# Stripe attention on one core: x of the row pairs is blocked in DRAM and turned by DMA, output stores choose their queue, and the order of steps is a new one

## The chip, the cores and the metric

The kernel runs on one core of one Trainium2 chip. The metric is the device time of one execution, in microseconds; the time before is the median of three runs. A profile is a separate execution, which gives each instruction of each engine with its start and duration: TensorE (PE, its weight loads PEld), VectorE (DVE), ScalarE (ACT), GpSimd (POOL) and the queues of SyncE (SP) and ScalarE (ACTq) that issue DMAs.

## The reference

An image of 224 x 224 positions with 96 channels is projected to q, k and v. The first 48 channels attend within horizontal stripes of 8 rows, the last 48 within vertical stripes of 8 columns; each stripe has 8 x 224 = 1792 tokens, and there are 28 stripes each way. Both results are put together and projected by wo.

```python
qkv = jnp.einsum('bhwc,cd->bhwd', x, wqkv)          # x: 1, 224, 224, 96
q, k, v = qkv[..., :C], qkv[..., C:2*C], qkv[..., 2*C:]
qh = q[..., :C2].reshape(B * nh, sw * W, C2)         # horizontal stripes, C2 = 48
ah = softmax(einsum('bqc,bkc->bqk', qh, kh) * C2 ** -0.5)
oh = einsum('bqk,bkc->bqc', ah, vh).reshape(B, H, W, C2)
...                                                  # qv, kv, vv, ov: the same with vertical stripes
o = concatenate(oh, ov)                              # written as a sum of two padded arrays
return jnp.einsum('bhwc,cd->bhwd', o, wo)
```

All arrays are bfloat16.

## The kernel before

The 56 stripes are worked in 28 pairs P: pairs 0 to 13 are horizontal (row pairs, phase 0), 14 to 27 vertical (phase 1). The two stripes w of a pair share the partitions: one stands on rows 0 to 63 of QT and KT, the other on rows 64 to 127.

**One pair.** The queries come in four chunks of 512, 512, 512 and 256, the keys in 14 tiles of 128. A score tile is 128 keys x 512 queries of both stripes (in the last chunk 256 keys x 256 queries), 1024 columns over two PSUM banks; a pair has 49. For 41 of them ACT takes the exponential out of PSUM into a tile `PT` (`emit_qk`, activation at L798; scores by `qk_fn`, L635). The other eight go another way (`emit_s`, L648): DVE and POOL work out the exponential by polynomials in 16-bit numbers (L836, L838, L841 on DVE, L848 to L852 on POOL), through buffers `qb`. `emit_pv` (L661) multiplies each `PT` with V into a PSUM bank; a column of ones in V gives the sums. When a chunk is complete, DVE copies it to `OT_sb` (L815).

**Work in between ("fills").** Matmuls with a DVE eviction each, through a ring of four PSUM banks:
- `prep_fills(P)` prepares the next pair from `xT_sb[P % 2]`, x with channels on the partitions and a row of ones at row 96. In phase 0 come first four T fills: each turns eight blocks of 112 tokens from `x_sb` by TensorE (L437, two transposes a block, so 16 matmuls), and DVE copies the bank into `xT_sb` (L443), where it also brings the tokens into the order of 8 x 8 blocks that the vertical phase needs. Then four K fills (L454, L459), one small QB fill (L483, L487), four Q fills (L454, L470) and three V fills (L501, L508). The first K fill needs all four T fills.
- `fin_fills(P)` multiplies `OT_sb` with wo and divides by the sums (L537, L544, L552 in phase 0, into `Ph_sb`; L573, L580, L585 in phase 1, which add `Ph_sb` and write `out_sb`).

**x.** `plan_x` (phase 0) loads a pair's x in four DMAs into `x_sb`, which lies in the memory of `out_all`; it is issued when the last T fill of the pair before has read `x_sb` (`emit_fill`). `keep_x` stores the turned x of each horizontal pair to `xt` in DRAM; in phase 1 `plan_x` loads a vertical pair's x from there, already turned. `x_sb` has a 97th column of ones, so that the row of ones is turned with it. Pair 0 has a way of its own, with x in `x0_sb` and steps written out one by one (`t_lead`, `lead_pe`, `lead_ev`).

**Output.** Each of the 392 DVE results of phase 1 (L585) is stored by a DMA of 24 KB, issued on SP (`emit_evict`). Once the last exponential has been put into the program, stores go by turns to SP's and ACT's queue (`tail_q`).

**Order.** The program is written as one list of steps, `ORDER`, a string for each pair: q is a score tile for ACT, 1 and 2 the two passes of a tile of DVE and POOL, v a PV step, k the next prep fill, f the next fin fill. PE runs them in exactly this order. A planner inside the kernel (`dve_step`, `pool_step`, with constants such as `D_ACT` and `D_H`) decides from modelled times in which order DVE and POOL take what PE hands them, and which bank and buffer each step gets. `x_t[P]` is the time from which the planner takes a pair's x to be there. `S.commit` and `dma` append each instruction with the semaphores that it must wait for. `queue_prep(P)` is called at the first score tile of pair P - 1: it issues that pair's DMAs on SP and puts the prep fills of pair P in their queue. SP works strictly in the order of issue: an instruction that waits holds all that stand behind it.

The lines that issue and choose:

```python
        for c in "".join(ORDER):
            if c == "q":
                do_q()
            elif c in "12":
                do_s(c)
            elif c == "v":
                do_v()
            else:
                do_fill(c)
```

Of the kernel before, what the change touches and what calls it, by code (L numbers as in the profile page):

```python
# [5 lines left out]
BF16 = mybir.dt.bfloat16  # L6
FP16 = mybir.dt.float16
FP32 = mybir.dt.float32
# [24 lines left out]
SEMD, SEMP, SELF, SEMX = 0.15, 0.10, 0.19, 0.05  # L33
D_H, D_SQ, D_AF, D_ML = 0.608, 1.9, 1.03, 2.08
# [9 lines left out]
    "kkqqkkkq1qkkq1qq1kqvqkvvq1vqvkqkq1qkvq2vqkq1vqvvqvq2qvkq2qkvqkvvvq1qvkvqkvvq1kqv2qkqvkvq2qvvkqkq2vqvkqv1qvvkqvv2qkqvv",  # L44
    "fqkkqkfqvq1vvkqq2vvvq1vvqvvqv2qvvqvvq1q2vqkvvq1qvkvqffqvkqv1qkvvqkqv2qvkqkvq1qvvqk2qvvvq1qvvffqvvq2qkvqkvq2vkqvq2vvqv1qvvqkvfq",
    "v1qvvq1vqvvqkvqkq2vqvvq1vqvkq1qvq1vqvvvqvkq2qvvvq1vqkkqvv2qkvqvfqv2qvvq2vkqvvkq2qvvkvqkq1vvq2qvvvkqffqvvkqv2qvvvqkqvkvfqffqvvkvq2qvvvv",
    "1qvvq1qvvvq1vqvvqkqvkq1qfvvqv1qkqkq2qfvkqkqfkqvq2vqfvvq1qvvvqvvq2vkqvq1vvq2qvvvvq2qvvkvq2qvvvkvq1qvvvkq2qvvkqkqkvvkqffqvvkvvq2fqv",
    "vvq1qvvvq1vqkvq1qkvqvvqfvqkqv1qkq2fqvvqvkvq2vqv1qvq2vkqq1vqvkqvvvqkvq2kqvvq1qvkvqkqkkqfvq2qvkqvvkq2vqv1qkvqv1qvvvqvfqv1qvv",
    "2qvvq1vvqvqvvkq2qvkqkvqffqvvvvq2qvvkqv1q1qvvvq2qvkvqkvq1vqvvvqv2qvqkkvqv1qkfqvkvqkfqvvq1vqv2qvvq2vqvfqv2qvkqkvvq2qvvkqv1qkvqvvkqffvv",
    "q2qvkvqfvq1vqvvq1fqvvvqvvq1qvkqv2qfqvvq1vvq1vqkqvvqkq2vqv1qvq2vqkvkqkvqkvq2vqvvq2kvq1qvvkvq2qvvkvq1qvkvqkvvqf2qvvvqvkqkvfqv2qkv",  # L50
    "vq1qv1qvvqvvfqvqfkqkqk2qvqkvfqv1qvvq1vqv1qvvqvkqvfqvvq2vvkqvq2vqvkq2vvvq2qvvvkvq1qvkfqv2qvfqkvqkvkq1qvvkqvkq2vqv1qvvvq1qvvkvq2qvkv",
    "vvq1qvvvvqvqkfqkvqvvq1q2qvq2vqkqvfq1vqvkqfqvv2qvqv1qkvvqvqvkqvkvqvkq2qvvfqvvq1qkfqvvkq1vqv2qvfqvkqvkvq2qvkvqkvqk1qvvvvq2qvvvk",
    "vq2qkqkv1qvq1qvvkqvfqvvvvq1qvvv1qvqf2qvvvvq2qvkvq1qvkqvvqvv2qkqkvvkqvq1kqvvffqvvq2vqvkq1qvvkq2qvvkq2qkvqvkkqvvq2fqvvvqv1qfvqvvkq1",
    "fqvvkvqq2vkvqvq1vvqvvq2qvqvvq1qv2qkqkq1q1qvvqvvvfqfqvkvvqkvkqfvkvqq2kvv1qqvvkvvq2qvvkvq2qvvvq1vvq2qkvqkkvqv2qvvqvfqvvkq1qkvvq1vfqvv",
    "q2vqv1qvkqvqkqkvqv1qvq2vqv2qvkqfvqfvvq1qvvkqkkvqv1qvvqvkqvvq2kq1qvvvq2qvkqv2qvvfqfvqkqkkvq1qvkvqvkq2vfqvkqvvvqf1qvvvq2vvq2vvq",
    "ffqvvvq1vqvkfqvvqv1qvkqvqvvq2vqkvq1qkfqvvqkq1qvvkq2vqvkqkfqkvvq2vqkvq1kqvvqkqvvfqvvqv2qvvq1vvqkq2vqv2qkvvq1qvkvvq2qvvvfqkvqkvvvq1f",
    "qvvvvq2vqvqfvvvq1vq1qvqvvq1qv2qvvqkv1qvkq2qvvq1vqvkqqvvqvv2qvfqkqvk1q2qvvq2qfvqvkvq2qkvvq1qvv1qkqkvvq1qvkkqvvvq1qkvvvqvvq2v",
    "qvfqvv2qvfqvvq1vqvvq1vqv2qvvqvkq1vqvkvqvvqvkqkvfqv2qvvq2vqvvq2vqvfqkvq1vqkvqvkq2vqvkq1qvv2qvkqvkq1qvvvq1kqvvkqvfqv2qvvq2vqv1qv",
    "vvqvvvqffqvvvvq2qvv1qvvqv1qkqkqvkqfkqvfqvkqvkq2qkqv2qvvq1vqvkqvvqkvq2qvvq1fqvvqfvvqv2qvqv1qfvvq2qvkqvq1vqvkvq1qvfqkvvvq2qvvv",
    "q2fqvvvqvfqvvqvv1qqvvqvv1qfqvvq2vvqq1vvq2qkvkqkqv2qkvvq1qkvvqvvq2qvvq1fqvvkqvqkvq1vfqvvq2vqkqvv2qvqkkqv2qvvvvq2qvvvkq1qkvvq1vf",  # L60
# [3 lines left out]
    "1qvvvqvvq2qfqv1qvvqvvvq1vqv1qvvqvvqvfq1qvvqvvkq2qvv2qvvq2qvkqkvkqv2qkvqkq1vqvkq2vqvkq2vfqvqkvqfvvqv2qvvq1qvvkqvkqfvq2qvvfqk",  # L64
    "vqv2qvvq1q1qvvvqvvq1fqvqvvvvq1qvvkvqkvq2qkvfqvkqvvq2vvqffqvvqvvvqv2qkqf2qvqvvkq1qvvvqvqkvq1vqvkq2vqkkqkvq1qvvvqfkqvv2qvvq1vq",
    "1qvvqv2qfvqvq1vqvvqvvvqv1qfqq2vqvvkq2vqvq1fqvvvq2vqvkqv1qkvqvvqkvvqv1qkq2kqvvq2qvvkq1qkvvq1vqfkqvq2vqvkqkvq2vqvvkq1qvv1q",
    "fqvvvqvvq1qvvfqvvq2vqv1qvvqv2qvvq2vvqv2qkq1qvvfqvqvkqvvvq1vqv2qvvq2vqvvq1fqvvqkvkqvfqvkvq2qkvvvq1qfvvvq2qvvkqkqkvvvq2qvkvvqkvq1kqv",
    "ffqvvqfqvvqv1qvvvqvvq1vqvqv2qkvvqkvqfvqv2qvvq1vqv2qvvkqkvfqvqkvq1vqvkqvvqv1qfqv2qvqv1qvq2vfqvvq2vqkqkvvqv1qvq2vqkkvq1qvkqvkv",
    "q2fqvvvqv1qqvvfqvqvvvq1qvvvq1vqkvqkq1vvqvqvv2qkqkvvq2vqv2qvq1vvqfqk2qvvqkqkkvq2qvvfqvvvq2qvv1qfqvkvqvvq2qvkvvq1qvvvkq1qfvvqfvk",
    "qvfqvq2vvq1qvqvvvq1qvvvqfvq2qvvvq1qvvkqkvq2vqv2qvfqkvqkvvq2vvqvvq2qv1qfqvvvqkqv1qvfqvvvq2qvkqkq1vkqkqvq2vfqvvvq1qvvkvq1qkvk",  # L70
    "vq2qfvqvvq1vvqqvv1qvvqv1qvvq2q2qfvqvvq1vvqvqvvq2vfqvvq1vqvqv1fqvqvvvq2qvvq2vfqvvvq2vqfvfqvqvvfqvvffqvvfqvq2vfqvvvq2fqvvfqvvqvqfffvvvvvvfff",
# [101 lines left out]
def bass_standalone__window_attn_cswin__vision_kernel(  # L173
# [28 lines left out]
    with es:  # L202
# [19 lines left out]
        xT_sb = [sb(f"xT_sb{i}", [C + 1, 2, NTOK], BF16) for i in range(2)]  # L222
# [12 lines left out]
        x_sb = out_all[0:TH, 0:2 * NTH * (C + 2)].rearrange("p (w k c) -> p w k c", w=2, k=NTH)  # L235
# [18 lines left out]
        for b in range(2):  # L254
            for w in range(2):
                SEMS[f"x{b}{w}"] = sem(f"s_x{b}{w}")
            SEMS[f"out{b}"] = sem(f"s_out{b}")
            SEMS[f"xt{b}"] = sem(f"s_xt{b}")
        dma_tot = {k: 0 for k in SEMS}
# [71 lines left out]
        pool_now(["xone"], lambda e: e.memset(x_sb[:, :, :, C:C + 1], 1.0), 0.25)  # L331
# [27 lines left out]
        xt = nc.dram_tensor("xt_dram", [WB, C, NTOK], BF16).ap()  # L359

        def ph_of(P):
            return 0 if P < NPH else 1

        def plan_x(P):
            for w in range(2):
                if ph_of(P) == 0:
                    i = 2 * P + w
                    src = x_flat[i * NTOK:(i + 1) * NTOK, :].rearrange("(k p) c -> p k c", p=TH)
                    for hf in range(2):
                        dma("sp", [], [("x", w, hf)], x_sb[0:TH, w, hf * FTH:(hf + 1) * FTH, 0:C],  # L370
                            src[:, hf * FTH:(hf + 1) * FTH, :], f"x{w}{hf}")
                else:
                    b = P % 2
                    dma("sp", [("xt", i) for i in range(NPH)], [("xT", b, w)], xT_sb[b][0:C, w, :],
                        xt[2 * (P - NPH) + w], f"x{w}{b}", lat=4.5)
# [16 lines left out]

        flags = set()
# [31 lines left out]
        def prep_fills(P):  # L425
# [3 lines left out]
            for w in range(2 if ph == 0 else 0):  # L429
                for hf in range(2):  # L430
                    k0 = hf * FTH

                    def pe_fn(e, bk, w=w, k0=k0):
                        bkb = bk.bitcast(BF16)
                        for j in range(FTH):
                            for a, z in HALVES:
                                ins = e.transpose(bkb[a:z, j * TH:(j + 1) * TH], x_sb[0:TH, w, k0 + j, a:z], ident[0:TH, 0:TH])  # L437
                        return ins

                    def d(e, bk, w=w, hf=hf):  # L440
                        src = bk.bitcast(BF16)[0:C + 1, 0:FTH * TH].rearrange("c (r bc dw) -> c r bc dw", r=RPF, dw=8)
                        dst = xT_sb[b][0:C + 1, w, :].rearrange("c (bc r dw) -> c r bc dw", r=SW, dw=8)[:, hf * RPF:(hf + 1) * RPF, :, :]
                        return e.tensor_copy(dst, src)  # L443
                    pd, dd = 0.42, 0.53
                    T.append(fill("B", pd, pe_fn, [("x", w, hf), "ident", "xone"],
                                  [(dd, d, [], [("xT", b, w)], None)], [], ("T", P, w, hf)))
            for kind, L in (("k", K), ("q", Q)):
                for c in range(NCH):
                    q0, qs = CH_Q0[c], CH_SIZES[c]

                    def pe_fn(e, bk, kind=kind, q0=q0, qs=qs):
                        for w in range(2):
                            lw = w_sb[:, wblk(P, "k"), :] if kind == "k" else wq_sb[ph][b][:, w, :]
                            ins = e.matmul(bk[64 * w:64 * w + 64, 0:qs], lhsT=lw, rhs=xT_sb[b][:, w, q0:q0 + qs],  # L454
                                           start=True, stop=True)
                        return ins
                    if kind == "k":
# [5 lines left out]
                        needs = [("T", P, w, hf) for w in range(2) for hf in range(2)] if c == 0 and ph == 0 else []  # L463
                        if P >= 2:
                            needs = needs + [("PV", P - 2)]
# [26 lines left out]
            for k0 in range(0, 2 * NKT, VS):  # L492
# [12 lines left out]
                def d(e, bk, k0=k0, n=n):  # L505
# [5 lines left out]
                              [("T", P, w, hf) for w in ws for hf in range(2)] if ph == 0 else [], ("V", P, k0)))  # L511
# [81 lines left out]

        tail_q = [0]
# [167 lines left out]
        plan_x(1)  # L762
        p_left = {}

        def queue_prep(P):
            if P <= NPH:
                keep_x(P - 1)
            if P == NPH:
                plan_x(P)
            if NPH <= P < NP - 1:  # L770
                plan_x(P + 1)
            T, K, QB, Q, V = prep_fills(P)
            fl = T + K + [QB] + Q[:1] + V + Q[1:]
            if P in (1, NPH - 1):
                fl = [wqT_fill(P // (NPH - 1))] + fl
            prep_q.extend(fl)
            p_left[P] = len(T)
# [9 lines left out]
        def emit_fill(f, bi):  # L787
            S.commit("pe", 0.0, f["pe_dur"], f["pe_dur"] + L_FILL, lambda e, fn=f["pe_fn"], bk=bank(bi): fn(e, bk),
                     f["reads"], [("bank", bi)], fresh=[("bank", bi)])
            g = f["gives"]  # L790
            if g[0] == "T":
                p_left[g[1]] -= 1
                if p_left[g[1]] == 0 and g[1] + 1 < NPH:
                    plan_x(g[1] + 1)
# [23 lines left out]
        def emit_evict(f, bi, k):  # L818
# [374 lines left out]
```

## Time and profile before

| | us |
|---|---|
| median of three runs (1088.88 to 1089.72) | 1088.9 |
| the profiled execution | 1089.64 |
| span of its trace, first to last instruction | 1087.8 |
| ACT busy (98%) | 1067.8 |
| PE busy (97%) | 1057.2 |
| DVE busy (96%) | 1044.7 |
| POOL busy (88%) | 954.9 |
| first exponential of the pairs starts (from the span's start) | 9.10 |
| last exponential ends | 1078.36 |

The span is what the trace shows of the engines; the time of an execution has 1.84 us around it. Busy time counts an engine as busy whenever at least one of its instructions is under way, and neighbouring instructions overlap (a matmul or an activation is begun before the one before has ended), so a busy share says less than the step from one start to the next. TensorE's granted clock was full throughout the pairs. The DMA engines were busy for about a fifth of the span.

Of the DMAs, by line, with the median time from issue to landing: the loads of x in phase 0 (52 of 168 KB) took 3.0 us, the stores of turned x (26 of 336 KB, in pieces of 128 bytes) 5.4, its loads in phase 1 (28 of 336 KB) 3.9, the output stores (392 of 24 KB) 1.9.

### The profile page before, as it was taken

Reading aid. Unit: us, or ns where it says so; the run is one execution under the profiler, and the core shown is the slowest. Engines: PE = TensorE matmul, PEld = TensorE weight load, DVE = VectorE, ACT = ScalarE, POOL = GpSimd, SP = SyncE. Lnnn points to the kernel's source line nnn. Section 1 sums busy time; section 2 is a strip of 40 time slices with the busy share of each in tenths; the row PEclk is TensorE's granted clock in tenths of the full one; section 3 lists DMA queues with packets and bytes.
Section 4 is the critical chain, followed back from the end, with each engine's and each line's share of the span. In section 5 each row is a group of like instructions: output and inputs, shape, how many; then the busy total and the mean of one; then the engine's idle time right before and its main releaser. Section 6 shows DMA issues by size and latency. Waiting matters only on the chain. (4 is left out here: it accounts for less than half of the span.)

```text
span 1087.8 us, 36152 instructions
## 1 busy us (share of the span) xinstructions
PE 1057.2 (97%) x14928; PEld 428.0 (39%) x14928; DVE 1044.7 (96%) x2298; ACT 1067.8 (98%) x1159; POOL 954.9 (88%) x597
## 2 busy tenths in 40 slices
PE   9999999999999999999999999999999999999996
PEld 4433444444343444444334333333333333333332
DVE  8999999999999999999999999999999999999997
ACT  8999999999999999999999999999999999999996
POOL 7999788899888988987999888998987999798894
PEclk9999999999999999999999999999999999999998
DMA  5413023202302311311011111112111111211102
GB/s 95 67 25 53 16 38 52 48 14 46 53 15 40 53 33 22 54 28 52 2 27 29 29 45 45 41 22 49 40 42 28 45 39 20 49 43 21 25 19 39
DMA packets 183805, 40.97 MB, mean 38 GB/s; under 512 B 180408, under 2 KB 180952, under 8 KB 183640
## 3 DMA queue, kind: packets, MB, share of 16 engines
q1 hardware_dynamic: 182520, 38.17, 18.2%
q8 instruction: 117, 1.92, 0.7%
q10 hardware_dynamic: 1120, 0.49, 0.2%
q14 instruction: 48, 0.39, 0.1%
HBM read 19.36 MB, written 19.27 MB: 36 GB/s over the span
## 5 line engine op out<-in xcount | busy, mean ns | idle before, releaser
L798 ACT ACTIVATE PT<-ps 128x1024 bf16<-128x1024 f32 x1148 | 1063.5, 1064 | 6.9 <-PE ps L635 4.4
L635 PE MATMUL ps<-QT_sb,KT_sb 49*64 49x512 bf16 (+1 forms) x5420 | 477.6, 362 | 13.9 <-ACT PT L798 8.2
L661 PE MATMUL ps<-PT,V_sb 128*49 128x512 bf16 (+1 forms) x3136 | 459.8, 361 | 0.3 <-DVE PT L841 0.2
L848 POOL TENSOR_TENSOR PT<-qb 128x1024 f16<-128x1024 f16 x168 | 316.6, 1893 | 71.2 <-DVE qb L836 29.0
L852 POOL TENSOR_TENSOR PT<-PT,qb 128x1024 f16<-128x1024 f16 x168 | 355.6, 2126 | 8.9
L841 DVE SCALAR_TENSOR_TENSOR PT<-ps,PT 128x512 uint16<-128x512 f32 x448 | 291.2, 682 | 12.9 <-PE ps L648 7.0
L836 DVE TENSOR_SCALAR qb<-ps 128x512 f16<-128x512 int16 x448 | 291.1, 682 | 10.1 <-PE ps L648 7.2
L635 PEld LDWEIGHTS ps<-QT_sb,KT_sb 49*64 49x64 bf16 x5420 | 144.8, 104 | 286.0 <-ACT PT L798 254.9
L661 PEld LDWEIGHTS ps<-PT,V_sb 128*49 128x49 bf16 x3136 | 133.5, 103 | 201.1 <-issue 158.8
L851 POOL TENSOR_SCALAR PT<-PT 128x1024 f16<-128x1024 f16 x168 | 175.3, 1043 | 14.3
L648 PE MATMUL ps<-QT_sb,KT_sb 50*64 50x512 bf16 (+2 forms) x1792 | 178.8, 389 | 5.7 <-DVE PT L841 1.5
L850 POOL TENSOR_TENSOR PT<-PT 128x1024 f16<-128x1024 f16 x56 | 106.0, 1893 | 20.3 <-DVE PT L838 13.3
L585 DVE SCALAR_TENSOR_TENSOR out_all<-ps,rc,Ph_sb 128x96 bf16<-128x96 f32 x392 | 96.6, 307 | 0.4
L648 PEld LDWEIGHTS ps<-QT_sb,KT_sb 50*64 50x64 bf16 (+2 forms) x1792 | 51.1, 104 | 64.7 <-DVE qb L836 14.4
L838 DVE SCALAR_TENSOR_TENSOR PT<-ps,qb 128x512 f16<-128x512 int16 x112 | 72.8, 680 | 0.1
L815 DVE CAST OT_sb<-ps 113x512 bf16<-113x512 f32 x112 | 68.9, 615 | 1.0 <-PE ps L661 0.2
L470 DVE CAST QT_sb<-ps 128x512 bf16<-128x512 f32 (+1 forms) x111 | 67.5, 614 | 0.9 <-PE ps L454 0.3
L459 DVE TENSOR_SCALAR_CACHE_REDUCE KT_sb<-ps 128x512 bf16<-128x512 f32 x108 | 64.4, 615 | 0.5 <-PE ps L454 0.2
L552 DVE TENSOR_TENSOR Ph_sb<-ps,rc 128x480 bf16<-128x480 f32 (+1 forms) x84 | 51.9, 617 | 1.4
L508 DVE CAST V_sb<-ps 128x480 bf16<-128x480 f32 (+1 forms) x84 | 50.5, 619 | 1.4 <-PE ps L501 0.9
L454 PE MATMUL ps<-xT_sb,w_sb 97*64 97x512 bf16 x224 | 40.8, 365 | 0.3 <-DVE PT L838 0.2
L454 PE MATMUL ps<-xT_sb,wq_sb 97*64 97x512 bf16 x224 | 40.7, 363 | 0.0
(63 smaller groups left out, 393.1 us busy)
## 6 DMA issues: line engine op xcount, KB each, us to landing
xT_sb<-xt_dram SPq DMA_DIRECT2D x28, 336.0 KB, 3.9
out_dram<-out_all SPq DMA_DIRECT2D x386, 24.0 KB, 1.9
out_all<-in_x_dram SPq DMA_DIRECT2D x52, 168.0 KB, 3.0
xt_dram<-xT_sb SPq DMA_DIRECT2D x26, 336.0 KB, 5.4
xt_dram<-xT_sb SPq DMA_DIRECT2D x4, 168.0 KB, 4.8
Ph_sb<-in_x_dram SPq DMA_DIRECT2D x2, 168.0 KB, 3.4
Ph_sb<-in_x_dram ACTq DMA_DIRECT2D x2, 168.0 KB, 3.7
out_dram<-out_all ACTq DMA_DIRECT2D x6, 24.0 KB, 1.9
```

Source lines behind the costliest of these rows:

```text
L454: ins = e.matmul(bk[64 * w:64 * w + 64, 0:qs], lhsT=lw, rhs=xT_sb[b][:, w, q0:q0 + qs], start=True, stop=True)
L585: return e.scalar_tensor_tensor(out_sb[b][:, w, kt, :], bk3[:, s, 0:C], rc[ri][:, s:s + 1], Ph_sb[:, kt, j, :], ALU.mult, ALU.add)
L635: ins = e.matmul(bank(SETS[s] + w)[64 * kh:64 * kh + 64, i * t["qs"]:(i + 1) * t["qs"]], lhsT=KT_sb[b][64 * w:64 * w + CA, kt * 128 + 64 * ...
L648: ins = e.matmul(bank(bp[w])[64 * kh:64 * kh + 64, 0:512], lhsT=KT_sb[b][64 * w:64 * w + nr, kt * 128 + 64 * kh:kt * 128 + 64 * kh + 64], ...
L661: ins = e.matmul(bank(pb)[64 * w:64 * w + CA, 0:t["qs"]], lhsT=V_sb[b][:, w, kt, :], rhs=PT[slot][:, ca:ca + t["qs"]], start=st and i == 0 ...
L798: S.commit("act", 0.0, D_ACT, None, lambda e, s=s, slot=slot: e.activation(PT[slot][:], ps[:, 512 * SETS[s]:512 * SETS[s] + 1024], ACTF.Ex ...
L836: fn, reads, writes = lambda e: e.tensor_scalar(q, low16(bi), m, a, ALU.mult, ALU.add), bk, qk
L841: fn, reads, writes = lambda e: e.scalar_tensor_tensor(y.bitcast(U16), bank(bi), 128.0, y.bitcast(FP16), ALU.mult, ALU.add), bk + ptk, ptk
L848: sq = lambda e: e.tensor_tensor(y, q, q, ALU.mult)
L850: return [("pool", D_SQ, lambda e: e.tensor_tensor(y, y, y, ALU.mult), yk + ["pser"], yk)]
L851: af = lambda e: e.tensor_scalar(y, y, PB, 128.0 * PA, ALU.add, ALU.mult)
L852: ml = lambda e: e.tensor_tensor(y, y, q, ALU.mult)
```

## The change

- **x of pairs 1 to 13.** `block_x` copies a stripe from DRAM to DRAM (`xp`), so that the tokens stand in the order of 8 x 8 blocks, in pieces of 1536 bytes. `load_x` loads it into `x_sb`, now 128 partitions x 14 blocks x 128 columns for each stripe, of which the DMA fills 96; the other 32 are ones, written once. `turn_x` turns it with one DMA transpose for each stripe, from `x_sb` into `xT_sb`, whose tile now has 128 rows. The T fills are gone, and with them what waited for them (`t_t`, `t_n`, `p_left`).
- **When.** `queue_prep` issues, on SP, the transposes of a pair one pair ahead, its load before that and its block copy before that. Pairs 1 and 2 are issued in the lead; pair 1's transposes stand on SP behind the loads of wo.
- **Stores.** `tail_q` is replaced by two modelled times, `tm["sp"]` and `tm["aq"]`, each store counting `D_ST`; after the last exponential a store goes to ACT's queue if that one is free earlier by them.
- **Order.** 22 of the 28 strings of `ORDER` are new; each has 41 q as before.
- The share of tiles between ACT and the other two engines (`KINDS`, `KIND_OF`), all score, PV, K, Q, V and output matmuls, and all DVE and POOL operations on them stay. Counted in the built programs, PE has 832 matmuls fewer (the transposes), DVE 52 copies fewer; SP has 26 block copies, 26 loads and 26 transposes where it had 52 loads.

```diff
-        xT_sb = [sb(f"xT_sb{i}", [C + 1, 2, NTOK], BF16) for i in range(2)]
+        xT_sb = [sb(f"xT_sb{i}", [128, 2, NTOK], BF16) for i in range(2)]
...
-        x_sb = out_all[0:TH, 0:2 * NTH * (C + 2)].rearrange("p (w k c) -> p w k c", w=2, k=NTH)
+        x_sb = out_all[:, 0:2 * NKT * 128].rearrange("p (w k c) -> p w k c", w=2, k=NKT)
...
-        pool_now(["xone"], lambda e: e.memset(x_sb[:, :, :, C:C + 1], 1.0), 0.25)
+        pool_now(["xone"], lambda e: e.memset(x_sb[:, :, :, C:].rearrange("p w k c -> p (w k) c").bitcast(FP32), pair_of_ones), 0.5)
...
+        xp = nc.dram_tensor("xp_dram", [2, 2, WB, SW, 8 * C], BF16).ap()
...
+        def block_x(P):
+
+            for w in range(2):
+                src = x[0, (2 * P + w) * SW:(2 * P + w + 1) * SW].rearrange("r (b d) c -> b r (d c)", d=8)
+                dma("sp", [], [("xp", P % 2, w)], xp[P % 2, w], src, f"xp{P % 2}{w}")
+
+        def load_x(P):
+            for w in range(2):
+                src = xp[P % 2, w].rearrange("b r (d c) -> (b r d) c", d=8).rearrange("(k p) c -> p k c", p=128)
+                dma("sp", [("xp", P % 2, w)], [("x", w)], x_sb[:, w, :, 0:C], src, f"xl{w}")
+
+        def turn_x(P):
+            b = P % 2
+            for w in range(2):
+                reads, writes = [("x", w), "xone"], [("xT", b, w)]
...
+                def fn(eng, w=w):
+                    return eng.dma_start_transpose(xT_sb[b][:, w, :].rearrange("c (k p) -> c k p", p=128),
+                                                   x_sb[:, w, :, :].rearrange("p k c -> p (k c)")).then_inc(SEMS[f"xr{b}{w}"], 16)
+                S.ops["sp"].append((d, fn, False))
...
+        block_x(1)
+        block_x(2)
         flags = set()
...
-            for w in range(2 if ph == 0 else 0):
-                for hf in range(2):
-                    k0 = hf * FTH
...
-                    T.append(fill("B", pd, pe_fn, [("x", w, hf), "ident", "xone"],
-                                  [(dd, d, [], [("xT", b, w)], None)], [], ("T", P, w, hf)))
...
-        plan_x(1)
-        p_left = {}
+        load_x(1)
+        turn_x(1)
 
         def queue_prep(P):
-            if P <= NPH:
-                keep_x(P - 1)
-            if P == NPH:
-                plan_x(P)
-            if NPH <= P < NP - 1:
+            if P == 1:
+                keep_x(0)
+                load_x(2)
+                keep_x(1)
+                block_x(3)
+            elif P == 2:
+                turn_x(2)
+                load_x(3)
+                keep_x(2)
+                block_x(4)
+            if 2 <= P < NPH - 1:
+                turn_x(P + 1)
+                if P + 2 < NPH:
+                    load_x(P + 2)
+                keep_x(P + 1)
+                if P + 3 < NPH:
+                    block_x(P + 3)
+            elif P >= NPH - 1 and P + 1 < NP:
                 plan_x(P + 1)
...
                 if ia[0] >= len(act_seq):
-                    q = ("sp", "actq")[tail_q[0] % 2]
-                    tail_q[0] += 1
+                    tm["aq"] = max(tm["aq"], tm["act"])
+                    if max(done, tm["aq"]) < max(done, tm["sp"]):
+                        q = "aq"
+                tm[q] = max(done, tm[q]) + D_ST
...
-                    x_t[P + 1] = st + 11.0 if P + 1 == NPH else 0.0
+                    if P > 0:
+                        x_t[P + 1] = st + XR2 if P == 1 else 0.0
```

More of the change, by code (lines that the diff above doesn't have):

```diff
@@ L33 @@
 SEMD, SEMP, SELF, SEMX = 0.15, 0.10, 0.19, 0.05
+D_ST = 0.64
+XR1, XR2 = 19.0, 5.0
 D_H, D_SQ, D_AF, D_ML = 0.608, 1.9, 1.03, 2.08
@@ L48 @@
[L48 to L55, printed above, removed]
@@ new lines, in turn_x @@
+        def turn_x(P):
+            b = P % 2
+            for w in range(2):
+                reads, writes = [("x", w), "xone"], [("xT", b, w)]
+                if P == 2:
+                    writes += ["xT1"] + [("xT", 0, w, hf, h2) for hf in range(2) for h2 in range(2)]
+                d = {k for k in S.deps("dma", reads, writes) if k[0] != f"xr{b}{w}"}
+                dma_tot[f"xr{b}{w}"] += 16
+                tok = (f"xr{b}{w}", dma_tot[f"xr{b}{w}"])
+                S.done[tok] = 0.0
+                def fn(eng, w=w):
+                    return eng.dma_start_transpose(xT_sb[b][:, w, :].rearrange("c (k p) -> c k p", p=128),
+                                                   x_sb[:, w, :, :].rearrange("p k c -> p (k c)")).then_inc(SEMS[f"xr{b}{w}"], 16)
+                S.ops["sp"].append((d, fn, False))
+                S.note(tok, reads, writes)
@@ L364, in plan_x @@
         def plan_x(P):
+            b = P % 2
             for w in range(2):
-                if ph_of(P) == 0:
-                    i = 2 * P + w
-                    src = x_flat[i * NTOK:(i + 1) * NTOK, :].rearrange("(k p) c -> p k c", p=TH)
-                    for hf in range(2):
[L370 to L375, printed above, removed]
+                dma("sp", [("xt", i) for i in range(NPH)], [("xT", b, w)], xT_sb[b][0:C, w, :],
+                    xt[2 * (P - NPH) + w], f"xr{b}{w}")
@@ L453, in pe_fn @@
                             lw = w_sb[:, wblk(P, "k"), :] if kind == "k" else wq_sb[ph][b][:, w, :]
-                            ins = e.matmul(bk[64 * w:64 * w + 64, 0:qs], lhsT=lw, rhs=xT_sb[b][:, w, q0:q0 + qs],
+                            ins = e.matmul(bk[64 * w:64 * w + 64, 0:qs], lhsT=lw, rhs=xT_sb[b][0:C + 1, w, q0:q0 + qs],
                                            start=True, stop=True)
@@ L462, in prep_fills @@
                         rd = ["w0z", "w"]
-                        needs = [("T", P, w, hf) for w in range(2) for hf in range(2)] if c == 0 and ph == 0 else []
-                        if P >= 2:
-                            needs = needs + [("PV", P - 2)]
+                        needs = [("PV", P - 2)] if P >= 2 else []
                         L.append(fill("B", 0.216 * qs / 512, pe_fn,
@@ L510, in prep_fills @@
                               [(0.065 + n * 0.05, d, ["vones"], [("V", b, k0)], None)],
-                              [("T", P, w, hf) for w in ws for hf in range(2)] if ph == 0 else [], ("V", P, k0)))
+                              [], ("V", P, k0)))
             return T, K, QB, Q, V
@@ L789, in emit_fill @@
                      f["reads"], [("bank", bi)], fresh=[("bank", bi)])
[L790 to L794, printed above, removed]
         def emit_qk(tl, s, slot):
@@ L816, in emit_ot, with emit_evict @@
                      [("bank", pb)], [("OT", P % 2, c)])
-        def emit_evict(f, bi, k):
+        def emit_evict(f, bi, k, done):
             st = f["chain"][k]
@@ L856, in bass_standalone__window_attn_cswin__vision_kernel @@
         NB = len(RING)
-        tm = dict(pe=8.43, act=7.83, end=0.0, dve=8.74, pool=10.9, mode="B", run=9, fin=False)
+        tm = dict(pe=8.43, act=7.83, end=0.0, dve=8.74, pool=10.9, sp=0.0, aq=0.0, mode="B", run=9, fin=False)
         set_free = [8.05, 7.4]
@@ L907, in dve_step @@
                 f, k = d["fill"], d["stage"]
-                emit_evict(f, d["bank"], k)
+                emit_evict(f, d["bank"], k, done)
                 if k == len(f["chain"]) - 1:
@@ L911, in dve_step @@
                     g = f["gives"]
-                    if g[0] == "T":
-                        t_t[g[1]] = max(t_t.get(g[1], 0.0), done)
-                        t_n[g[1]] = t_n.get(g[1], 0) + 1
-                    elif g[0] == "K":
+                    if g[0] == "K":
                         k_t[g[1:]] = done
@@ L1092, in do_fill @@
                     assert P < 2 or n_done[P - 2] == 49
-                    if P > 0 and ph_of(P) == 0:
-                        wait_for(lambda: t_n.get(P, 0) == 4)
-                        r = max(r, t_t[P])
                 elif g[0] == "QB":
@@ L1101, in do_fill @@
                     r = max(r, kb_t[P])
-                elif g[0] == "V" and ph_of(P) == 0:
-                    r = max(r, t_t.get(P, 0.0))
             b, t = get_banks(1)
```

58 lines of the change are left out of this document (27 added, 31 removed).

## The prediction

> **What bounds the kernel now.** I read the page's busy shares first, then busy time by stretches, then the groups, the waits and the chain at the end.
>
> ```profile
> PE 1057.2 (97%) x14928; PEld 428.0 (39%) x14928; DVE 1044.7 (96%) x2298; ACT 1067.8 (98%) x1159; POOL 954.9 (88%) x597
> ...
> L798 ACT ACTIVATE PT<-ps 128x1024 bf16<-128x1024 f32 x1148 | 1063.5, 1064 | 6.9 <-PE ps L635 4.4
> ```
>
> Three engines are above 95%, so shares alone decide nothing. ACT runs 1148 exponentials (L798), a number that the change leaves. Each overlaps the next, so what counts is the step from start to start. The chain of waits shows the smallest one, 0.90 us:
>
> ```profile
> 1074.58 0.68 ACT PT L798
> ...
> 1075.48 0.68 ACT PT L798
> ...
> 1076.38 1.97 ACT PT L798 x2
> ```
>
> Busy time by stretch (columns: stretch, length, then each engine's busy us and instructions). I cut where the last transposes end: pairs 0 to 12 prepare a following row pair (533 exponentials), the rest does not (615), and then comes the tail after ACT's last end.
>
> ```profile
> 9.10:509.69 500.59, 493.80 (x7370) 207.94 (x7366) 482.38 (x938) 495.74 (x533) 441.45 (x269) 1.00 0.24 41
> 509.69:1078.36 568.67, 554.92 (x7480) 214.44 (x7476) 554.65 (x1322) 567.74 (x616) 507.73 (x301) 1.00 0.15 34
> 1078.36:1087.80 9.44, 0.90 (x16) 0.42 (x16) 2.51 (x12) 0.00 (x0) 0.00 (x0) 0.64 0.26 48
> ```
>
> One exponential costs 500.59/533 = 0.939 us in the first stretch and 568.67/615 = 0.925 in the second. Above 0.90 there are 20.9 us in the first and 15.2 in the second: ACT is the bound, and this is all that its feeding still costs. PE feeds it and is the tighter one in the first stretch: it idles 6.8 us of 500.59 there, 13.8 of 568.67 in the second. When ACT does stand still, it waits for PE's score matmuls (L635, 4.4 us above).
>
> **The transposes that leave.** PE loses 832 matmuls (52 groups of 16) and DVE 52 copies:
>
> ```profile
> L443 DVE COPY xT_sb<-ps 97x896 bf16<-97x896 bf16 x52 | 31.8, 616 | 1.7 <-PE ps L437 0.5 <-PE ps L635 0.5
> ...
> 19.80 0.58 PE L437 MATMUL ps<-ident,out_all 112*64 112x112 bf16 x16
> 20.31 0.41 PE L635 MATMUL ps<-QT_sb,KT_sb 49*64 49x512 bf16 x4
> ```
>
> From the start of a group to the next group's start PE gives it 0.51 us here, 0.41 and 0.52 at the next two: 0.48 x 52 = 25 us of PE, 32 us of DVE, two of the four ring banks' turns with them. The gain on ACT is bounded by 0 (if the order alone makes the 20.9 us) and 20.9. Without its transposes a pair of the first stretch has the second stretch's PE work: the same K, Q, V and output matmuls (L537 and L573 have 784 each in 14 pairs). So the nearest row is the second stretch's step: 533 x (0.939 - 0.925) = 7.9 us by the unrounded numbers. DVE has less than there: L552 and L544 cost 51.9 and about 15 us in 14 pairs, 4.8 a pair, while L585 and L580 cost 96.6 and about 16, 8.0 a pair. At the second stretch's step about 13 us above 0.90 would be left in the first; I credit DVE's 3.2 us a pair with 2.0 of them (0 and 13 are its ends). Sum here: 9.9 us gained.
>
> **The DMAs that come.** Each pair's x now goes DRAM to DRAM (two block copies of 336 KB), DRAM to SBUF (two loads, padded to 128 columns in SBUF), and SBUF to SBUF turned (two transposes of 448 KB); the two stores of the turned x stay. SP issues eight where it issued six. The rows to price them:
>
> ```profile
> xT_sb<-xt_dram SPq DMA_DIRECT2D x28, 336.0 KB, 3.9
> ...
> xt_dram<-xT_sb SPq DMA_DIRECT2D x26, 336.0 KB, 5.4
> ...
> q1 hardware_dynamic: 182520, 38.17, 18.2%
> ```
>
> No row is a transpose. By size a long-piece load gives 3.9 x 448/336 = 5.2 us, a store in pieces of 128 bytes 5.4 x 448/336 = 7.2; if every 2-byte element were a packet at the 17.4 ns that q1's took (18.2% of 16 x 1087.8 us over 182,520), 229,376 of them on 16 engines would take 250 us. I take 5.2, since both sides lie in SBUF rows of 256 bytes or more and pieces of that size behave in the rows like the first two. From pair 3 on the transposes are issued one pair ahead, some 38 us before the first matmul that reads them, so 5 to 7 us cost nothing; the cover is a whole pair. Pair 2 has nine score tiles, about 8.5 us. Only pair 1 is short. SP's queue in the lead:
>
> ```profile
> 10.46 1.23 SPq L276 DMA_DIRECT2D woh<-in_wo_dram  x2
> ...
> 14.08 1.13 SPq L276 DMA_DIRECT2D wov<-one_sb  x2
> 15.25 2.28 SPq L276 DMA_DIRECT2D out_all<-in_x_dram  x4
> ```
>
> The wo loads wait for POOL's memsets until 10.46 and all later issues stand behind them, so the loads of pair 1 still go out at 15.3. The first lands at 15.3 + 3.9 = 19.2, the second about 1.6 later, 20.8, by the issue spacing and a shared 16 engines; the second transpose lands at 20.8 + 5.2 = 26.0. Counted in the new order, pair 1's first K matmul stands behind the 18th score tile, which at 0.90 a step is free to start at about 23.9, the K matmul at 24.3. All of PE's queue (scores, PV) stands behind that K. The stall is 1.7 us, and PE is about 0.5 ahead of ACT, so 1.2 us are lost. Ends: 0 (landing by 24.8) and 3.2 (7.2 us per transpose).
>
> The four block copies at the start are issued behind the first x loads and wst, while SP would wait for 10.46 anyway; I take 0, with 1 us as upper end if they slow wst, for which POOL now waits 1.1 us. That wait also hides the larger memset of ones. The mid load of pair 14 moves a pair earlier and waits for the last store of turned x; only later x loads stand behind it on SP, since output stores begin a pair later: 0.
>
> [...]
>
> **The stores.** At the end SP's queue is late:
>
> ```profile
> 1080.70 1.26 ACTq L276 DMA_DIRECT2D out_dram<-out_all  x2
> 1080.99 5.10 SPq L276 DMA_DIRECT2D out_dram<-out_all  x8
> ```
>
> DVE's last output is written at 1080.99, ACT's queue is done at 1081.96, SP's at 1086.09, and the span ends 1.7 us later. A store costs SP 5.10/8 = 0.64 us. The new rule could hand stores to ACT's queue, but in the built order ACT's list again ends with six and SP's again has 386, in the same alternation: the rule alone moves nothing. The new order does: with 20, 15 and 10 exponentials to go, 35, 30 and 21 SP stores are left before, and 30, 22 and 20 after, six instead of seven behind the last one. A first-in first-out queue at 0.64 us a store and 0.904 a step ends 2.2 us earlier. Gain 2.2; ends 0 and 4.1 (1086.09 - 1081.96). In the second stretch work and waits stay and only the order differs: 0, within 3 us either way, a fifth of its 15.2.
>
> **Sum.** -9.9 - 2.2 + 1.2 = -10.9 us on a span of 1087.8: 1076.9. The profiled execution took 1089.64, 1.84 more than its span; the median of the three runs, 1088.9, lies 0.74 below it. Forecast: 1088.9 - 10.9 = 1078.0.
>
> **Rivals.**
> - The transposes come late for pairs 1 and 2. For it: the lead's queue has no slack. At 7.2 us each and one after the other pair 1 stalls 24.3 to 20.8 + 14.4, less 0.5: 10 us at most; 3 to 10 us over the forecast's 1.2 gives 1080 to 1087. Against it: only two of 13 pairs lack cover.
> - PE is not relieved where it counts: the 20.9 us come from the order's bursts, as the second stretch, without transposes, still has 15.2. Then -2.2 + 1.2 gives 1087.9, no change. Against it: the step differs between the stretches as PE's idle does.
> - The transposes are cut so fine that the DMA engines (or SP, which issues them) become the bound, slower than before. A pair's x takes 0.24 x 38.5 = 9.2 us of all engines now, so about 28 us are free; 458,752 elements a pair at 17.4 ns a packet on 16 engines fill that with pieces of 35 bytes. At 32 bytes: 31.2 + 9.2 + 1 for the block copies = 41.4 us a pair against 38.5, and 13 x 2.9 = 38 us more, less 2.2: 1124. Single elements give 499 us a pair, over 7 ms. Against it: rows of 256 bytes can move whole, at 3.9 us a pair.
> - The relieved DVE closes most of the 13 us and the order gains in the second stretch: below 1070.
>
> **How the numbers follow.** Forecast 0.76, late transposes 0.08, no relief 0.05, DMA bound 0.07, more than expected 0.04. The range: low 1070, the DVE credit at 7 instead of 2 and the second stretch's 3; high 1086.5, most of the late case. It leaves out about 0.15. A measurement tells 0.2% (2.2 us) from no change: faster 0.76 + 0.08 + 0.04 = 0.88, same 0.05, slower 0.07.
>
> **What would show it.** In the profile after: a step of at most 0.925 up to pair 12; ACT's largest gap, if any, between 24 and 28 us, released by xT_sb's transposes; transposes landing in 4 to 8 us; SP's last store about 2 us after where ACT's queue ends, not 4. Wrong: a first stretch still at 0.939, SP or DMA waits in front of K matmuls in every pair, or a DMA share near 1 in the first half.

## The result, and the profile after

The changed kernel's median over 20 runs is 1083.64 us, against 1089.47 us for 20 runs of the kernel before: a difference of 5.8 us. Ratios and their 95% intervals here go by the means of the runs and leave out runs more than 1.5% above the fastest of their kernel (here those of 1093.41 and 1095.35 us; the other 18 end at 1089.67), while medians and ranges take in all: the ratio is 0.9938 (0.9919 to 0.9957). What stands out is the spread. The 20 runs of the kernel before lie between 1088.88 and 1090.77; those of the changed one between 1076.39 and 1095.35. Its profiled execution took 1083.81 us, with a span of 1082.0.

The same stretches as before, by the same cut (the 534th exponential, the end of the last one). Columns: stretch, its length, busy us and instructions of PE, PEld, DVE, ACT and POOL, granted clock, DMA share, GB/s. The changed kernel:

```profile
8.34:508.25 499.91, 487.58 (x6538) 185.35 (x6536) 459.62 (x886) 491.84 (x533) 444.89 (x275) 0.98 0.49 80
508.25:1075.39 567.14, 555.38 (x7484) 213.39 (x7480) 554.58 (x1322) 566.71 (x616) 505.96 (x299) 1.00 0.15 34
1075.39:1082.00 6.61, 0.90 (x17) 0.42 (x16) 2.53 (x12) 0.00 (x0) 0.00 (x0) 0.80 0.30 56
```

The first stretch, from which the forecast took nearly all its gain, is as long as before (499.91 against 500.59) although PE has 832 matmuls fewer and DVE 52 instructions fewer in it. The tail is 2.8 us shorter, the second stretch 1.5, and the first exponential started 0.76 us earlier in this execution. The granted clock is no longer full in the first stretch. Cut finer, with the same columns:

```profile
8.34:24.80 16.46, 15.28 (x228) 5.34 (x226) 15.79 (x29) 16.13 (x17) 14.62 (x21) 1.00 0.68 107
24.80:27.43 2.63, 0.80 (x10) 0.40 (x14) 1.04 (x3) 1.09 (x2) 2.63 (x2) 1.00 0.97 157
27.43:30.00 2.57, 2.21 (x20) 0.41 (x12) 1.95 (x5) 2.57 (x3) 2.41 (x3) 0.61 0.90 133
30.00:43.00 13.00, 13.00 (x88) 3.38 (x86) 8.66 (x19) 8.84 (x10) 12.01 (x9) 0.55 1.05 165
43.00:53.56 10.56, 10.54 (x191) 4.41 (x190) 9.51 (x18) 10.56 (x12) 9.70 (x6) 1.00 0.98 144
```

PE stands still first (0.80 of 2.63 us busy), then it is busy almost without a pause at about half the clock and issues 88 matmuls in 13 us where the next 10.56 us have 191. ACT, fed by it, works 8.84 of 13 us. Pair 0 took 45.2 us from its first exponential to the next pair's, the pairs of the first stretch behind it 37.5 to 38.1, except pair 7 with 39.7. PE's timeline shows where it began (start, length, instruction, count; in brackets the idle time before and what ended it), and the halved clock in the length of the same group of four score matmuls, 0.41 us at first and 0.64 afterwards:

```profile
24.30 0.41 PE L642 MATMUL ps<-QT_sb,KT_sb 49*64 49x512 bf16 x4
26.63 0.41 PE L465 MATMUL ps<-xT_sb,w_sb 97*64 97x512 bf16 x2 [1.93 <-DMA xT_sb<-out_all]
...
28.51 0.64 PE L642 MATMUL ps<-QT_sb,KT_sb 49*64 49x512 bf16 x4 [0.36 <-ACT PT L812]
```

The K matmul of pair 1 (L465) waited 1.93 us for the transposes. On SP they were issued at 18.87 and 22.14, when their loads had landed (18.85 and 22.12), and the second landed at 26.5. Their median from issue to landing, in the page's list of DMA issues, is 4.8 us:

```profile
xT_sb<-out_all SPq DMA_TRANSPOSE x26, 4.8
```

Pair 7, some 2 us longer than its neighbours, shows the same pattern: a gap of 0.74 us at 298.25, then 3.4 us at half the clock from 301.1.

### The profile page after: what moved, and what is told of

The parts are those of the page before. It is cut to its first block, busy times and chain, and to the rows that moved or that the text cites. A ratio compares the mean times of both kernels' runs of the same rounds, so it can differ in the third digit from the quotient of the medians.

```text
span 1082.0 us, 34436 instructions
## 1 busy us (share of the span) xinstructions
PE 1050.6 (97%) x14096; PEld 403.5 (37%) x14096; DVE 1021.5 (94%) x2246; ACT 1062.8 (98%) x1159; POOL 956.4 (88%) x597
## 5 line engine op out<-in xcount | busy, mean ns | idle before, releaser
L668 PE MATMUL ps<-PT,V_sb 128*49 128x512 bf16 (+1 forms) x3136 | 466.3, 364 | 0.1
L465 PE MATMUL ps<-xT_sb,w_sb 97*64 97x512 bf16 x224 | 41.5, 371 | 2.0 <-DMA xT_sb<-out_all 1.9
L465 PE MATMUL ps<-xT_sb,wq_sb 97*64 97x512 bf16 x224 | 41.3, 368 | 0.1
```

What stands on the lines that cost most here:

```text
L668: ins = e.matmul(bank(pb)[64 * w:64 * w + CA, 0:t["qs"]], lhsT=V_sb[b][:, w, kt, :], rhs=PT[slot][:, ca:ca + t["qs"]], start=st and i == 0 ...
```

## The experiments

**Pair 1's x earlier.** SP issues pair 1's load and transposes right behind its block copies, ahead of the loads of wo, which aren't needed until pair 0's output.

```diff
         block_x(1)
+        load_x(1)
+        turn_x(1)
         block_x(2)
...
-        load_x(1)
-        turn_x(1)
```

> Edit: SP issues pair 1's load and transposes right behind pair 1's block copies, ahead of pair 2's block copies and the loads of wo; nothing else moves. Theory: in the changed kernel pair 1's second transpose lands at 26.5 us, PE stands idle for 1.9 us in front of pair 1's first K matmul (24.7 to 26.6), and TensorE's granted clock is then halved for 13.7 us (28.0 to 41.7); pair 0 takes 45.2 us instead of 37 to 38. Without the wait: transposes land before 20 us, granted clock 1.00 from 8 to 50 us, pair 0 near 38 us, 1075 to 1077 us in most runs, and the spread of the runs (1076 to 1095) shrinks below 3 us. Rival A, DMA traffic: the DMA engines were busy 0.9 to 1.05 from 25 to 53 us and this slows the first pairs; then pair 0 stays at 43 to 45 us and the time at 1081 to 1085. Rival B, PE has so little work without transposes that the clock is halved anywhere, as for 3.4 us at 301 us behind a gap of 0.74 us: the stall goes, but the runs still spread from 1076 to 1090.

Measured: 1076.34 us, ratio 0.9895 (0.9879 to 0.9910); four runs between 1075.99 and 1076.45, one at 1081.79 with a mean clock of 0.992. The second transpose landed at 17.5, PE didn't wait, pair 0 took 38.6 us. Stretches of this kernel, with the columns of before:

```profile
9.00:501.14 492.14, 481.38 (x6538) 184.55 (x6536) 458.69 (x886) 490.80 (x534) 444.48 (x273) 1.00 0.50 82
501.14:1068.04 566.90, 555.29 (x7484) 213.10 (x7480) 554.54 (x1322) 566.53 (x616) 505.97 (x299) 1.00 0.15 34
1068.04:1074.20 6.16, 0.90 (x18) 0.42 (x16) 2.52 (x12) 0.00 (x0) 0.00 (x0) 0.73 0.30 56
```

Two calls moved forward in the order of issue are worth 7.3 us of the median. The DMA share in the first stretch is the changed kernel's (0.50), and between 30 and 43 us the DMA engines are as full as there (1.00 against 1.05), at full clock and full pace:

```profile
30.00:43.00 13.00, 12.82 (x190) 5.21 (x191) 12.45 (x26) 13.00 (x16) 12.68 (x9) 1.00 1.00 163
```

So rival A, DMA traffic that slows the engines, falls. Unedited again, it gave 1076.26 us (1075.9 to 1076.6, four runs), ratio 0.9885 (0.9872 to 0.9898):

> The first experiment again, unedited: is its outlier (1081.8, one of five) part of it? Theory: the one gap of 0.81 us at 292 us sometimes halves the clock: again about one run in five above 1080, the others at 1076.0 to 1076.6.

No outlier this time: one in nine over both. This version beats both kernels.

**PE kept busy through the wait.** The transposes stay late, but 12 dummy matmuls of 512 columns on constants run ahead of the waiting one, into the PSUM bank that it is about to write.

```diff
         def emit_fill(f, bi):
+            if f["gives"] == ("K", 1, 0):
+                busy_pe(bi, 12, 512)
```

> Edit: the changed kernel, with 12 matmuls of 512 columns on constant data in front of pair 1's first K matmul, into the bank that it is about to write; they don't wait for x. The transposes stay late. Theory (PE's idleness halves the clock): PE is busy through the wait, the clock stays 1.00 from 8 to 50 us, only the delay itself is left: up to 2.6 us of matmuls where it stood 1.9, 1077 to 1080 us. Rival A (DMA traffic): no change, 1081 to 1085 with pair 0 at 43 to 45 us. If the delay itself costs all of the loss, through banks and buffers that run empty, pair 0 also stays above 43 us but with the clock at 1.00.

Measured: the profiled execution took 1077.82 us with a full clock from 25 to 43 us, as the theory has it, 1.5 us above the median of the early load. The second transpose landed at 25.8, and PE was busy through the wait (its timeline, then two stretches with the columns of before):

```profile
24.69 2.35 PE L809 MATMUL ps<-warm 128*64 128x512 bf16 x10
26.67 0.40 PE L465 MATMUL ps<-xT_sb,w_sb 97*64 97x512 bf16 x1
...
24.80:27.40 2.60, 2.60 (x14) 1.24 (x13) 0.74 (x2) 1.15 (x2) 2.60 (x2) 1.00 0.99 156
27.40:43.00 15.60, 15.11 (x206) 5.75 (x204) 14.65 (x29) 14.92 (x17) 15.11 (x11) 1.00 1.06 165
```

The median is 1081.52 (1077.82 to 1084.3), above the 1077 to 1080 expected: two runs of six had a mean clock of 0.992, two 0.996, and one was at 1080.99 with 0.998. The one profile shows that the late transposes cost about 2 us where the clock stays full (pair 0 took 40.7 us against 38.6); why the other runs lost more, a cover that is too short or something else, isn't shown.

**PE made to wait with nothing late.** The early-load kernel, in which pair 1's first K also waits for the exponential of the tile in front of it.

```diff
         def emit_fill(f, bi):
+            if f["gives"] == ("K", 1, 0):
+                f["reads"] = f["reads"] + pt_keys(act_seq[ia[0] - 1]["slot"])
```

> Edit: the first experiment's kernel (x of pair 1 is there early), in which pair 1's first K matmul also waits for the exponential of the score tile just in front of it. No DMA is late; PE stands idle for about 2 us at 24 us, as in the changed kernel. Theory (it is PE's idleness that halves the clock, whatever the cause): runs spread as in the changed kernel, 1078 to 1090 us, granted clock 0.985 to 0.998, pair 0 at 40 to 46 us. Rival (late or crowded DMAs do it): 1077 to 1079 in all runs at clock 0.998.

Measured: 1085.51 us (1080.16 to 1096.73), clock 0.985 to 0.996. No DMA is late here (the second transpose landed at 17.6), and the whole loss is back, with its spread; in the profile pair 0 took 51.6 us, more than the 40 to 46 expected. PE's timeline, and the stretches before and after 26.8 us of the profiled execution:

```profile
25.02 0.41 PE L644 MATMUL ps<-QT_sb,KT_sb 49*64 49x512 bf16 x4
26.87 0.64 PE L467 MATMUL ps<-xT_sb,w_sb 97*64 97x512 bf16 x2 [1.44 <-ACT PT L814]
```

```profile
23.39:26.80 3.41, 1.76 (x22) 0.46 (x14) 2.68 (x5) 3.22 (x4) 3.41 (x3) 1.00 0.94 141
26.80:57.50 30.70, 30.63 (x252) 8.97 (x252) 18.37 (x34) 20.14 (x20) 23.99 (x15) 0.50 1.04 170
```

A gap of 1.44 us bought 30.7 us of half clock here: PE was busy for 30.63 of them, and ACT for 20.14. So a waiting PE can bring the halved clock about with no late DMA, though not each time, as the next experiment shows.

**The changed kernel again**, for a second profile of its lead.

> The changed kernel again, unedited, for a second profile of its lead beside the next two. Theory: the time at which pair 1's second transpose lands differs from run to run by some us, and the half-clock stretch behind it with the phase in which the gap falls; so the landing lies at 25 to 30 us, there is a PE gap of 1 us or more in front of pair 1's first K matmul, and the runs again spread over more than 10 us from about 1077. [...]

Measured: 1083.51 us (1077.11 to 1089.12, 12 runs), ratio 0.9955 (0.9931 to 0.9979). In its profile (1078.56 us) the second transpose landed at 26.44, as in the two other profiles with this issue order (26.5 and 25.8), and not anywhere between 25 and 30 as I had expected. The gap was 1.24 us, and the clock stayed full behind it; only a stretch of 3.4 us at pair 7 was there, from 296.02 (PE's timeline, then the window that holds most of the gap and the one in front of the halving):

```profile
26.53 0.41 PE L465 MATMUL ps<-xT_sb,w_sb 97*64 97x512 bf16 x2 [1.24 <-issue]
...
22.95:26.36 3.41, 2.10 (x23) 0.62 (x22) 3.02 (x7) 3.41 (x4) 3.41 (x2) 1.00 1.12 190
292.60:296.02 3.42, 2.76 (x38) 1.35 (x38) 2.85 (x7) 3.00 (x5) 3.42 (x3) 1.00 0.02 5
```

In the three profiles the landing is steady; what the clock makes of the gap is not.

**The old order without the T steps.** The early-load kernel with the strings of the kernel before, minus the 52 T steps. It asks what the relief is worth without the search.

> Edit: the first experiment's kernel (transposes by DMA, early), but with the strings of ORDER of the kernel before, out of which only the 52 steps of the T fills of pairs 1 to 13 are taken. It shows what the relief of PE and DVE is worth without the new search. The prediction put all 9.9 us of the first stretch down to the relief and 0 to the search outside the tail: then pairs 0 to 12 take about 493 us as in the first experiment (492.1), the second stretch 568.7 as before, the tail 9.4 (old order of stores): 1080 us. Rival: the gain is the search's; old steps without T leave PE's gaps where they were: first stretch 498 or more, 1085 to 1088 us.

Measured: 1098.38 us (1094.99 to 1105.63), ratio 1.0091 (1.0062 to 1.0119): slower than before, with less work, and worse than both my numbers. The clock of the runs was 0.975 to 0.988. In the profile the halved stretches are at 284.9 (17.1 us) and 411.2 (6.8 us). The window in front of the first, and the stretch itself:

```profile
281.49:284.90 3.41, 2.37 (x36) 0.89 (x34) 3.07 (x8) 3.41 (x4) 3.33 (x3) 1.00 1.14 187
284.90:302.00 17.10, 16.93 (x128) 4.55 (x124) 9.97 (x19) 11.29 (x12) 12.89 (x8) 0.50 0.59 100
```

There is no long gap here, the longest is 0.51 us; the gaps are many, 1.04 us together. The eleven pairs of the first stretch that had the full clock took 421.3 us together, against 422.5 of the same pairs before and 416.1 in the early-load kernel. So at full clock the relief alone is worth about 1 us in 11 pairs, and the new order on top of it 5 more. What a new search would give with the transposes still on PE was not run.

**The old order with PE's work put back.** The strings of the kernel before, unedited; in each T step PE runs ten dummy matmuls (0.5 us), and DVE reads one column instead of making its copy.

```diff
+            for i in range(4 if ph == 0 else 0):
+                def pe_fn(e, bk):
+                    for j in range(10):
+                        z = 112 * (j % 4)
+                        ins = e.matmul(bk[0:64, z:z + 112], lhsT=warm[:, 0:64], rhs=warm[:, 0:112], start=True, stop=True)
+                    return ins
...
+                T.append(fill("B", 0.42, pe_fn, ["warm0", "warm"], [(0.1, d, [], [("dmy", i)], None)], [], ("T", P, i)))
```

> Edit: the early-load kernel with the unedited ORDER of the kernel before; in the 52 T steps PE runs 10 matmuls of 112 columns on constant data (about the 0.48 us that the transposes took of it), and DVE reads one column of the bank instead of the copy of 0.61 us. So against the kernel before only DVE's 32 us are gone, and against the old-order experiment (1098 us, clock halved behind stretches of 3.4 us in which PE was busy under 2.4) PE's work is back. Theory: PE's transposes kept the clock up in the old order; with PE as busy as before no stretch is halved (clock 0.997 or more in all runs), and the time is that of the kernel before or a little less, 1083 to 1088 us. Rival: the old steps are slow without T for another reason (planned times that no longer fit, DMA traffic): 1092 or more, with clock drops.

Measured: 1089.91 us (1089.35 to 1091.31, 11 runs), ratio 1.0012 (1.0003 to 1.0021), clock 0.998 or 0.999 in every run. First stretch:

```profile
8.91:511.21 502.30, 496.66 (x7058) 212.60 (x7053) 461.69 (x937) 496.77 (x533) 442.08 (x272) 1.00 0.43 81
```

DVE has 21 us of busy time less there than the kernel before, PE 3 us more (496.66 against 493.80), and the stretch is no shorter (502.30 against 500.59). Compared with the experiment above, 8.5 us of median were gained by putting the T steps back into the order with useless work for PE in them. The theory held on the clock; its time of 1083 to 1088 was missed by 2 us.

**PE's load back, DVE's load back, in the new order.** On the early-load kernel, in two kernels: 16 dummy matmuls in front of each K fill of pairs 1 to 13 (the edit below); and one more DVE copy in four fills of each of these pairs.

```diff
         def emit_fill(f, bi):
+            if f["gives"][0] == "K" and 1 <= f["gives"][1] < NPH:
+                busy_pe(bi, 16, 112)
```

> Edit: the first experiment's kernel, with 16 matmuls of 112 columns on constant data in front of each K fill of pairs 1 to 13 (52 groups, as many matmuls as the transposes that the change took from PE), results overwritten. No DVE work is added. Prediction's step (PE was the tighter one): the step of the exponentials in the first stretch goes back from about 0.92 to 0.935 or more, 7 to 10 us above the first experiment's time. Rival (DVE was what held ACT up): 0 to 2 us. Rival B (clock): fewer clock drops than in the first experiment, since PE is busier.

> Edit: the first experiment's kernel, with one more DVE copy (97 rows x 448 float32 from the fill's own bank, about 0.6 us) in front of the eviction of three K fills and one Q fill of pairs 1 to 13: 52 copies, 32 us of DVE, as the change took away; no PE work is added. Prediction's step: 0 to 2.5 us above the first experiment (the credit given to DVE was 2.0). Rival (DVE was the limit): 7 to 10 us.

Measured: 1112.95 us (1112.35 to 1121.07) for PE, ratio 1.0221 (1.0208 to 1.0234), and 1102.68 us (1091.58 to 1104.33) for DVE, 1.0099 (1.0061 to 1.0136). Both are far above what I expected. PE: 52 groups at 16 x 112 columns are some 40 us, 1.6 times what the transposes took (an estimate by columns from the dummies that ran with the late transposes: two of 512 columns took 0.59 us and ten 2.35, so 0.22 for each more), and 36.6 us came out: added work on PE shows nearly one for one. DVE: pairs 1 to 12, but for pair 3 with its halved clock (49.2), took 38.5 to 39.8 us where the early-load kernel has 37.6 to 38.5, and the two runs without clock loss (1091.58 and 1092.22) are 15 us above it for 32 us of copies. The rest is the clock again: the profile has halved stretches behind gaps of 1.06 and 0.70 us. Neither tells a limit of the kernel before, because the order wasn't searched anew for the added steps.

**Dummy matmuls at the gap in front of pair 8's QB**, four of 512 columns, on the early-load kernel. They were meant to fill the gap.

> Edit: the first experiment's kernel, with four matmuls of 512 columns on constant data in front of the QB fill of pair 8, where PE stands idle for 0.81 us at 292.4 us (in the changed kernel the clock was halved for 3.4 us behind that gap). If the gap is what now and then halves the clock, the outlier of the first experiment (1081.8 at clock 0.992) does not come back: all runs 1075.5 to 1077. If the outliers come from elsewhere: one run in five above 1080 as before.

> The experiment with the filled gap in front of pair 8's QB again, unedited. Theory: no run above 1078.5, median within 1 us of the early-load kernel's undisturbed runs. If runs above 1080 come here too, the gap at 292 us is not what makes the outliers.

Measured: 1077.01 us (1076.54 to 1077.85) and 1077.70 us (1077.28 to 1078.93), four runs each. The gap was not filled: the dummies (L809) wait for the PSUM bank as the QB fill did, until DVE has released it, so PE stands idle for 0.70 us in the first profile and 0.73 in the second, against 0.81 and 0.69 in the two of the early-load kernel:

```profile
292.41 1.05 PE L809 MATMUL ps<-warm 128*64 128x512 bf16 x4 [0.70 <-DVE PT L866]
293.30 0.51 PE L494 MATMUL ps<-ksum,wqT 128*64 128x4 bf16 x4
```

No run is above 1080 in eight, against one in nine without the dummies, but since the gap is still there this doesn't test whether it makes the outlier. The dummies cost 0.7 to 1.4 us.

## Why the prediction came out as it did

**The lead's stall (1.2 us in the sum).** The mechanism was right and its first numbers too: second transpose at 26.0 forecast, 26.5 measured; the wait 1.7, 1.93 measured. What failed is the step from the stall to its cost, "the stall is 1.7 us, and PE is about 0.5 ahead of ACT, so 1.2 us are lost". The cost took PE, once its wait is over, to go on at its old pace. In the profiled execution the wait was followed by 13.7 us at half the clock, and pair 0 took 45.2 us instead of 38.6. By the medians of the two kernels that differ in this order of issue alone the term is 7.3 us (7.25 in the pair that was run side by side later), not 1.2: 6.1 us more, where 1083.64 is 5.6 above the forecast of 1078.0. That the time still lies between 1070 and 1086.5 is in part luck: the upper end was set for transposes that land late by several us, and these landed 0.5 us later than forecast; the loss came by the clock, for which the sum has no term.

**The first stretch (-9.9).** In the changed kernel it is -0.7, a step of 499.91/533 = 0.938 us, which is the prediction's own sign of being wrong ("still at 0.939"). With the wait taken away it is 492.14 against 500.59: -8.5, a step of 0.923. (533 x the difference of the two steps is 7.7 us by the unrounded numbers, not 7.9, so the term should have read -9.7.) The size was close, but the reason that I gave, relief of PE and DVE at an unchanged order, isn't what the runs show. At full clock the old order gains about 1 us in 11 pairs from the relief; DVE's relief alone gains nothing (502.30 with PE's load in place). For the old order, then, the rival by which the 20.9 us come from the order's bursts is the one that fits. The gain came with the order that was searched for the relieved engines. In that order unplanned work on either engine costs time, 36.6 us for 40 on PE and 15 for 32 on DVE, which fits PE as the tighter engine there; for the kernel before it isn't shown.

**The second stretch (0).** -1.5 in the changed kernel, -1.8 with the early load: within the 3 us given.

**The tail (-2.2).** 6.61 us against 9.44, -2.8; the new order does leave SP less to catch up. "The rule alone moves nothing" doesn't hold for the old order: as built for the experiment without T steps, the rule gives ACT's queue eight stores instead of six, and the tail there is 7.93.

**The transposes.** Landing 4.8 us after issue, near the 5.2 taken from the long-piece loads. SP was held 1.5 to 3.4 us by a transpose, with a median of 1.9 over the 26, where a pair's two stores of turned x held it 4.0 us together in the kernel before (from 52.04). Pair 1's two transposes took 5.4 and 4.4 us from issue to landing, and PE waited. The third rival is excluded: the DMA share of the first stretch is 0.49, and the only wait of PE for a transpose is the 1.93 us of pair 1.

**The first rival** had the right place, and the time lies in its 1080 to 1087, but by another way. Only pair 1 was late, and by less than 2 us; what was dear is the clock behind the wait.

What I hadn't looked for at all is what speaks against the change: the trace of before shows a full clock throughout the pairs and a PE with 6.8 us of idle time in 500, and I read the second as a cost only. The halved stretches last 13.65 and 3.41 us in the changed kernel's profile (from 28.02 and 301.08), 3.4 in its second one, 30.7 with the added wait, 17.1 and 6.8 in the old order without T steps: all close to whole multiples of 3.41 us (4, 1, 1, 9, 5 and 2). PE was not idle throughout the 3.41 us in front of any of these six: it was busy, by the profile, for 1.48, 2.67, 2.76, 1.76, 2.37 and 2.33 us there, in the same order. Nor did the clock come back at once with a busy PE: one that was busy 30.63 of 30.70 us stayed at half. The phase in which a gap falls, which I took ahead of the changed kernel's second profile for what sets the price, is shown by no run. If such stretches of 3.41 us end where the clock changes, the gap of 1.24 us that cost nothing lies for the most part in one from 22.95 to 26.36 in which PE was busy 2.10 us, less than the 2.76 in front of the halving at 296.02 in the same profile.

**Open:** which gaps halve the clock; why it returns after 3.4 us in one case and after 30.7 in another; why three of the changed kernel's 20 runs (1083.5 to 1084.2) lost 7 us at a mean clock of 0.998 or 0.999. One profile hints at it without settling it: in the experiment with PE's load back the score matmuls have their halved length of 0.64 us in the lead, up to about 27 us, and 0.41 after, in an execution 8 us longer than its neighbours whose mean clock nevertheless reads 0.999.

## What to carry to other kernels

TensorE's own load may be what keeps its clock full, as in the two experiments with the old order (0.975 to 0.988 in the runs without the T steps, 0.998 or 0.999 with ten dummy matmuls in each): before work is taken from it, look for the stretches in which it would then pause, because a pause of a microsecond can cost ten (1.44 us of idle PE was followed by a pair 0 of 51.6 us instead of 38.6). A transfer that is a little late is priced by what the wait sets off, not by its length (1.93 us of wait stood in front of the 7.3 us by which the medians differ); where the cover is thin, change the order of issue first, which cost nothing here. And work that is removed from a fixed order of steps may gain little until the order is searched again.

## What the runs showed of the hardware that was not expected

- Six half-clock stretches in four profiles came behind windows of 3.4 us in which PE was still busy 43 to 81% of the time, and lasted 3.4 to 30.7 us with PE busy almost without pause. In the kernel before, whose longest PE gap in the pairs is 0.51 us, none came in its profile.
- The same program on the same data spread over 19 us (1076.39 to 1095.35, 18 of 20 over 13) where the kernel before spreads over 2, although the late transpose landed within 0.7 us of the same time in three profiles (25.8 to 26.5).
- An SBUF to SBUF transpose of 448 KB took 4.8 us from issue to landing, as long as a 336 KB load from DRAM in pieces of 192 bytes beside it (4.6), and no slowing of the engines shows: pairs 1 to 6 took 37.5 to 38.0 us with the DMA engines half busy, the pairs of the second stretch, without transposes, 37.5 to 38.3.
